# Planning the order of a fused attention and feed-forward kernel anew

## The chip, the cores and the metric

The kernel runs on one core of one Trainium2 chip. A core has five engines that run side by side and meet only through semaphores: TensorE (PE, matmuls into the accumulator memory, PSUM), VectorE (DVE), ScalarE (ACT), GpSimd (POOL) and SyncE (SP, which here issues every DMA). The metric is the device time of one execution in microseconds. The kernel before took 720.09 us, the median of three runs (719.34 to 721.42).

## The reference

Two stages follow each other; inputs and results are float32. B = 4, H = 8 heads, S = 1152 keys, D = 64, and the 1152 queries are averaged in pairs to 576.

```python
q_pool = q.reshape(B, H, S // 2, 2, D).mean(axis=3)
scores = (1 / np.sqrt(D)) * np.matmul(q_pool, k.transpose(0, 1, 3, 2))
scores = scores - np.max(scores, axis=-1, keepdims=True)
attn = np.exp(scores)
attn = attn / (np.sum(attn, axis=-1, keepdims=True) + 1e-09)
x = np.matmul(attn, v)             # heads side by side: (4, 576, 512)
h = np.maximum(x @ w_in, 0.0)      # (4, 576, 1024)
conv_out = conv_w[0] * h[t-1] + conv_w[1] * h[t] + conv_w[2] * h[t+1]
out = (h * sigmoid(conv_out)) @ w_out
```

## The kernel before

Heads are worked on in 16 pairs, four pairs to a batch. For a pair, keys, values and queries are loaded; GpSimd adds neighbouring queries; TensorE transposes keys and queries (L345, L350, L382, L392, into one of two accumulator buffers called `a`), and ScalarE copies them to `kt` and `qt`, the two heads on partitions 0 to 63 and 64 to 127. A DMA (L400) writes `qd`, the same queries with the two halves of the partitions swapped, so that a head's keys can be used from either half.

A score task (`scores`, L516) makes 128 queries by 1152 keys of one head in one of two buffers called `s`: 512 keys from one half of the partitions, 512 from the other, and the last 128. Each matmul in float32 is two instructions in the trace, so a task has six. VectorE takes the maximum (L528), ScalarE the exponential with its sum (L533), which frees the buffer. There are eight such tasks a pair, and a ninth (`m`) for the last 64 queries of both heads, with 64 by 64 blocks of the array. The exponentials, in `p`, are normalized and cut into a half-precision high part (ScalarE, L574) and low part (VectorE, L577), and a transposing DMA (L590) turns both. For the heads listed in `X32`, GpSimd normalizes instead (L607), TensorE transposes in float32 (L620) and ScalarE copies (L625). `values` multiplies by the values and sums over the keys: three half-precision products (L650) or one in float32 (L656) for every block of 128 keys, for 256 queries and then for 320; the list `BLOCK` gives the block of keys in which a row of values stands.

When a batch's four pairs are done, `feed` makes the first product (L690), rectifier (ScalarE), the three taps (GpSimd L699, VectorE L706), the gate, and `second` the second product (L749, and L755 for the last 64 rows). Its two parts of the tokens are interleaved with the next batch's attention. Weights come in through a chain of steps on VectorE, ScalarE and GpSimd.

The order in which every engine works is made by a planner. Each step is a `Task` with a key (its due time, in units of score tasks, from the table `AT`), an engine and a duration. `Plan.order` goes forward in time: of the steps that may begin, it takes the engine that is free first, and on it, of what could start within `LOOK` of the earliest, the one with the lowest key. `HOP` is the delay that it assumes between engines, `SWITCH` what a change of `mode` costs on TensorE, and steps with `port` set exclude each other. Tasks of one engine are then issued in that order, and the engine works through them strictly in turn.

## Time and profile before

| | |
|---|---|
| time of the runs | 719.34, 720.09, 721.42 us; median 720.09 |
| the profiled execution | 718.41 us, its span 716.6 us |
| TensorE, VectorE, ScalarE, GpSimd busy | 659.9, 551.2, 498.2, 177.1 us |
| TensorE's granted clock, mean over the span | 0.98 |
| DMA | 118.55 MB, its queue 79.8% of 16 engines' span |

The span is what the trace covers, from the first instruction to the last; the execution's own time lies around it. Busy time is a union: instructions of one engine that overlap count once. In the trace a matmul's record runs from its start to its modelled end, so the records of neighbours overlap.

### The profile page before, as it was taken

How to read it: one execution, taken by the hardware profiler on the slowest of the kernel's cores; microseconds unless marked ns; L12 is line 12 of the kernel's file. 1: busy time of each engine (PE TensorE's matmuls, PEld its weight loads, DVE VectorE, ACT ScalarE, POOL GpSimd, SP SyncE). 2: the span in 40 equal slices, each digit the busy share in tenths (PEclk: the TensorE clock that was granted, in tenths of full speed). 3: DMA queues.
4: the chain of work that ended last, by engine and by line, in shares of the span. 5: the costliest groups of instructions: out<-in, count | busy, mean ns of one | idle time of the engine just before them, and what ended most of it. 6: DMA issues, size and time to landing. Idle time of an engine off the chain costs nothing.

```text
span 716.6 us, 11043 instructions
## 1 busy us (share of the span) xinstructions
PE 659.9 (92%) x3992; PEld 398.6 (56%) x3992; DVE 551.2 (77%) x813; ACT 498.2 (70%) x810; POOL 177.1 (25%) x237
## 2 busy tenths in 40 slices
PE   4789889899998899999999998999999989999997
PEld 3445555556565545456665664456665655458743
DVE  2878887887889898868888999578888889864610
ACT  2887878876786777676876888567886868663310
POOL 2442453433433322011241212031141212001200
PEclk9999999999999899999999998999999999999999
DMA  5887695764468989989999999989999896873001
GB/s 155 221 178 179 167 212 132 166 167 118 113 141 173 233 151 190 209 186 202 200 183 221 193 182 223 193 172 175 220 181 209 161 187 144 171 168 74 1 30 37
DMA packets 311722, 118.55 MB, mean 165 GB/s; under 512 B 286556, under 2 KB 297332, under 8 KB 311668
## 3 DMA queue, kind: packets, MB, share of 16 engines
q1 hardware_dynamic: 311668, 117.85, 79.8%
q8 instruction: 31, 0.51, 0.3%
q14 instruction: 23, 0.19, 0.1%
HBM read 36.72 MB, written 4.72 MB: 58 GB/s over the span
## 4 chain that ended last, share of the span: by engine, by line
PE 68%; DVE 6%; ACT 5%; issue 2%; ACTq 0%; DVEq 0%
PE s L516 17%; PE a L690 17%; PE a L749 16%; PE a L650 12%; PE a L755 2%; DVE sm L528 2%; PE a L656 2%; DVE hl L577 2%; ACT p L533 2%; ACT hl L574 1%; PE a L620 1%; PE a L345 1%; PE a L426 1%; ACT pt L625 1%; PE a L382 0%
## 5 line engine op out<-in xcount | busy, mean ns | idle before, releaser
L528 DVE TENSOR_REDUCE sm<-s 128x1 f32<-128x1152 f32 x144 | 193.3, 1351 | 57.4 <-PE s L516 56.6
L533 ACT ACTIVATE p<-s,sm 128x1152 f32<-128x1152 f32 x144 | 175.4, 1219 | 49.4 <-DVE sm L528 41.3
L516 PE MATMUL s<-kt,qt 64*128 64x512 f32 (+3 forms) x512 | 184.0, 515 | 11.4 <-ACT p L533 10.7
L516 PE MATMUL s<-kt,qd 64*128 64x512 f32 (+2 forms) x448 | 177.9, 546 | 13.0 <-ACT p L533 11.5
L577 DVE SCALAR_TENSOR_TENSOR hl<-p,sm,hl 128x1152 f16<-128x1152 f32 (+1 forms) x124 | 176.9, 1437 | 11.8 <-ACT hl L574 10.7
L574 ACT ACTIVATE hl<-p,sm 128x1152 f16<-128x1152 f32 (+1 forms) x124 | 153.0, 1249 | 10.4 <-DVE sm L549 4.3
L690 PE MATMUL a<-x,wi 128*128 128x257 f32 (+1 forms) x512 | 140.1, 424 | 2.2 <-ACT pt L625 0.9
L749 PE MATMUL a<-wo,g 128*128 128x512 f32 x256 | 119.2, 607 | 0.6 <-ACT kt L354 0.6
L650 PE MATMUL a<-pt,v 128*64 128x256 f16 (+1 forms) x1458 | 118.2, 289 | 0.1
L516 PEld LDWEIGHTS s<-kt,qt 64*128 64x128 f32 (+1 forms) x512 | 70.8, 178 | 79.8 <-issue 59.1
L690 PEld LDWEIGHTS a<-x,wi 128*128 128x128 f32 x512 | 96.1, 194 | 33.9 <-issue 3.9
L699 POOL TENSOR_SCALAR g<-h,cw 128x255 f32<-128x255 f32 (+1 forms) x64 | 51.6, 809 | 231.2 <-ACT h L696 229.8
L516 PEld LDWEIGHTS s<-kt,qd 64*128 64x128 f32 (+1 forms) x448 | 65.8, 182 | 66.9 <-issue 44.2
L650 PEld LDWEIGHTS <-v 128*64 128x64 f16 x1458 | 90.7, 110 | 14.7 <-issue 5.2
L706 DVE SCALAR_TENSOR_TENSOR g<-h,cw,g 128x321 f32<-128x321 f32 (+1 forms) x128 | 66.8, 524 | 16.0 <-POOL g L699 14.6
L749 PEld LDWEIGHTS a<-wo,g 128*128 128x128 f32 x256 | 46.5, 192 | 50.7 <-issue 46.4
L696 ACT ACTIVATE h<-a 128x257 f32<-128x257 f32 (+1 forms) x64 | 26.2, 409 | 40.0 <-PE a L690 38.6
L656 PE MATMUL a<-pt,v 128*64 128x256 f32 (+1 forms) x180 | 48.6, 412 | 1.5 <-ACT pt L625 0.8
L625 ACT ACTIVATE pt<-a 128x384 f32<-128x384 f32 (+1 forms) x70 | 32.0, 477 | 17.5 <-PE a L620 16.8
L620 PE MATMUL a<-ident,p 128*128 128x128 f32 (+1 forms) x225 | 34.6, 275 | 5.1 <-ACT pt L625 2.4
L607 POOL TENSOR_SCALAR p<-p,sm 128x1152 f32<-128x1152 f32 (+1 forms) x25 | 32.1, 1285 | 28.9 <-DVE sm L549 23.1
L451 POOL TENSOR_SCALAR vs<-vs 128x1 f32<-128x1 f32 x16 | 9.3, 582 | 107.3 <-DVE vs L445 91.8
(68 smaller groups left out, 551.3 us busy)
## 6 DMA issues: line engine op xcount, KB each, us to landing
kin<-in_k_dram SPq DMA_DIRECT2D x16, 576.0 KB, 4.5
qin<-in_q_dram SPq DMA_DIRECT2D x32, 256.0 KB, 3.4
vin<-in_v_dram SPq DMA_DIRECT2D x11, 576.0 KB, 5.4
g<-in_moe_w_in_dram SPq DMA_DIRECT2D x8, 512.0 KB, 6.0
g<-in_moe_w_out_dram SPq DMA_DIRECT2D x8, 512.0 KB, 3.5
out_dram<-o SPq DMA_DIRECT2D x16, 256.0 KB, 2.5
qd<-qt SPq DMA_DIRECT2D x16, 160.0 KB, 3.4
pt<-hl SPq DMA_TRANSPOSE x135, 4.7
```

The costliest lines, as they stand in the source:

```text
L516: nc.tensor.matmul(out=w, lhsT=f, rhs=o.kt[r, e, c1:c2], start=True, stop=True)
L528: nc.vector.tensor_reduce(out=sm[:, e:e + 1], in_=runs(st[e]), axis=AX.XY, op=ALU.max, negate=True)
L533: nc.scalar.activation(out=p.tile().rearrange("p (a n) -> p a n", a=2), in_=runs(st[e]), func=AF.Exp, bias=sm[:, e:e + 1], scale=1.0, accu ...
L574: nc.scalar.activation(out=hl[rows, 0], in_=ps_[e][rows], func=AF.Copy, scale=sm[rows, 6 + e:7 + e])
L577: nc.vector.scalar_tensor_tensor(out=hl[rows, 1], in0=ps_[e][rows], scalar=sm[rows, 6 + e:7 + e], in1=hl[rows, 0], op0=ALU.mult, op1=ALU.s ...
L620: nc.tensor.transpose(w[:, (i - a1) * nq:(i - a1 + 1) * nq], ps_[e][rows, i * P:(i + 1) * P], ident[rows, rows])
L650: nc.tensor.matmul(out=to, lhsT=o.v[:, e, BLOCK[c], vc:vc + D], rhs=o.pt[y, e][:, hl * NC + c, 0:n], start=(c == 0 and j == 0), stop=(c == ...
L656: nc.tensor.matmul(out=to, lhsT=o.v[:, e, BLOCK[c]].bitcast(F32), rhs=p32.rearrange("p (a n) -> p a n", a=NC)[:, c, 0:n], start=(c == 0), ...
L690: nc.tensor.matmul(out=w[:, 0:n], lhsT=wi[:, j, f * P:(f + 1) * P], rhs=x.x[:, 255 * u:255 * u + n], start=(j == 0), stop=(j == KC - 1),)
L699: nc.gpsimd.tensor_scalar(out=g[:, f % 4, 0:tok], in0=h[:, 0:tok], scalar1=cw[:, f, 0:1], scalar2=1.0, op0=ALU.mult, op1=ALU.mult,)
L706: nc.vector.scalar_tensor_tensor(out=c, in0=h[:, t:t + tok], scalar=cw[:, f, t:t + 1], in1=c, op0=ALU.mult, op1=ALU.add)
L749: nc.tensor.matmul(out=w.tile(), lhsT=g[f // 4][:, f % 4, c:c + P], rhs=wo[:, f, :], start=(f == 0), stop=(f == FC - 1),)
```

## The change

The planner's table of durations is replaced, and with it the keys in `AT`. `HOP` goes from 0.12 to 0.19, a hop within TensorE from 0.03 to 0; the rule that two steps with `port` exclude each other is taken out; among the steps that could start, one of TensorE that stays in its mode counts as due 0.95 earlier. `HIGH` moves 16 of the high parts to GpSimd. `X32` gets one head of the eleventh pair. `values` is cut in two steps where it was cut in three.

A pair's keys are turned in nine transposes of 128 by 128: the 18 blocks of 64 columns of both heads are taken two by two, the ninth holding a block of either head. So `kt` has no second index, the second head's blocks stand in another order (`BLOCK` has one list a head), and the 128 last keys of the second head lie in the other half of the partitions than those of the first. The second head's score task therefore starts on partitions 64 to 127. The last queries are summed twice, side by side, and turned in one full transpose, so that they stand on both halves of the partitions; the swapped copy `qd` and its DMA leave them out, and the swap waits for the other queries alone.

```diff
-    HOP = 0.12
+    HOP = 0.19
...
-                at = max(t.ready, s[0], free.get(t.engine, 0.0), port if t.port else 0.0)
+                at = max(t.ready, s[0], free.get(t.engine, 0.0))
...
-                key=lambda c: (first[c[1].engine], c[1].rank),
+                key=lambda c: (
+                    first[c[1].engine],
+                    c[1].key - (AT["stay"] if c[1].engine == "PE" and c[1].mode == mode else 0.0),
+                    c[1].rank,
+                ),
...
-                hop = 0.03 if n.engine == t.engine and not t.dma else self.HOP
+                hop = self.HOP if n.engine != t.engine or t.dma else 0.0 if n.engine == "PE" else 0.12
...
-    "first_v": 1.35, "load": -15.29, "load_v": -7.7, "turn_k": -6.99, "turn_q": -4.19, "abs_v": -6.45,
...
+    "first_v": 1.88, "load": -3.54, "load_v": 0.5, "turn_k": -6.86, "turn_q": -6.9, "abs_v": -4.95,
...
+    "wi_step": 2.86, "wo": 31.13, "wo_step": 2.5, "stay": 0.95,
...
-HIGH = [0, 0, 0, 0, 0, 0, 0, 0, 0, 0, 0, 0, 0, 0, 0, 0]
-X32 = {(0, 0), (1, 0), (2, 0), (3, 0), (4, 0)}
+HIGH = [3, 0, 0, 0, 0, 0, 0, 3, 0, 1, 1, 4, 1, 0, 4, 2]
+
+BOTH = set()
+
+PARTS = 2
+X32 = {(0, 0), (1, 0), (2, 0), (3, 0), (4, 0), (10, 0)}
...
-    BLOCK = (0, 2, 4, 6, 8, 1, 3, 5, 7)
+    BLOCK = ((0, 2, 4, 6, 8, 1, 3, 5, 7), (2, 4, 6, 8, 0, 1, 3, 5, 7))
...
     r_vin = Ring("vin", 1, sb, [P, 2, NC, D], F32, lead=True)
     r_qin = Ring("qin", 1, sb, [P, 2, 2, 4, D], F32, lead=True)
     r_qm = Ring("qm", 1, sb, [P, 2, D], F32, lead=True)
-    r_kt = Ring("kt", 2, sb, [P, 2, K0], F32, lead=True)
+    r_kt = Ring("kt", 2, sb, [P, S], F32, lead=True)
     r_qt = Ring("qt", 2, sb, [P, K0], F32, lead=True)
-    r_qd = Ring("qd", 2, sb, [P, K0], F32, lead=True)
+    r_qd = Ring("qd", 2, sb, [P, K1], F32, lead=True)
     r_qs = Ring("qs", 1, sb, [P, 4, 2, D], F32, lead=True)
-    r_qms = Ring("qms", 1, sb, [P, D], F32, lead=True)
+    r_qms = Ring("qms", 1, sb, [P, 2, D], F32, lead=True)
     r_v = Ring("v", 2, sb, [P, 2, NC, P], F16, lead=True)
     r_p = Ring("p", 3, sb, [P, S], F32, lead=True)
     r_hl = Ring("hl", 4, sb, [P, 2, S], F16, lead=True)
...
             def turn(i=i, w=w):
-                if i < 2:
-                    for c in range(4):
-                        nc.tensor.transpose(
-                            w[:, c * P:(c + 1) * P], o.kin[:, i, 2 * c:2 * c + 2].rearrange("p c d -> p (c d)"), ident
-                        )
-                else:
-                    for e in range(2):
-                        nc.tensor.transpose(w[0:D, e * P:(e + 1) * P], o.kin[:, e, 8], ident)
+                rows = o.kin.tile().rearrange("p h c d -> p (h c d)")
+                for n, c in enumerate([range(0, 8, 2), range(10, 18, 2), (8,)][i]):
+                    nc.tensor.transpose(w[:, n * P:(n + 1) * P], rows[:, c * D:(c + 2) * D], ident)
 
             def keep(i=i, w=w):
-                if i < 2:
-                    nc.scalar.activation(out=o.kt[:, i, 0:K1], in_=w[:, 0:K1], func=AF.Copy)
-                else:
-                    nc.scalar.activation(
-                        out=o.kt[0:D, :, K1:K0], in_=w[0:D, 0:2 * P].rearrange("p (e n) -> p e n", e=2), func=AF.Copy
-                    )
-
-            t = add(k0 + AT["turn_k"] + i, "PE", 0.75 if i < 2 else 0.4, turn, after=lk,
+                n = K1 if i < 2 else P
+                nc.scalar.activation(out=o.kt[:, i * K1:i * K1 + n], in_=w[:, 0:n], func=AF.Copy)
+
+            t = add(k0 + AT["turn_k"] + i, "PE", 0.5 if i < 2 else 0.15, turn, after=lk,
                     uses=[o.kin] + ([o.kt] if i else []), takes=[w] if i else [w, o.kt])
             o.kts.append(
-                add(k0 + AT["turn_k"] + i + 0.1, "ACT", act(K1 if i < 2 else 2 * P), keep, after=[t],
-                    uses=[w, o.kt])
+                add(k0 + AT["turn_k"] + i + 0.1, "ACT", act(K1 if i < 2 else P), keep, after=[t], uses=[w, o.kt])
...
         def sum_m():
-            nc.gpsimd.tensor_tensor(out=o.qms.tile(), in0=o.qm[:, 0], in1=o.qm[:, 1], op=ALU.add)
+            for i in range(2):
+                nc.gpsimd.tensor_tensor(out=o.qms[:, i], in0=o.qm[:, 0], in1=o.qm[:, 1], op=ALU.add)
...
         def turn_m():
-            nc.tensor.transpose(wm[0:D, 0:P], o.qms.tile(), ident)
+            nc.tensor.transpose(wm[:, 0:P], o.qms.tile().rearrange("p i d -> p (i d)"), ident)
 
         def keep_m():
-            nc.scalar.activation(out=o.qt[0:D, K1:K0], in_=wm[0:D, 0:P], func=AF.Copy, scale=QSCALE)
+            nc.scalar.activation(out=o.qt[:, K1:K0], in_=wm[:, 0:P], func=AF.Copy, scale=QSCALE)
 
         def swap(e):
             h, g = slice(D - D * e, P - D * e), slice(D * e, D * e + D)
-            n = K1 if e else K0
-            nc.sync.dma_start(out=o.qd[h, 0:n], in_=o.qt[g, 0:n])
-
-        t0 = add(k0 + AT["sum_q"], "POOL", 0.95, lambda: sum_q(0), after=lq, uses=[o.qin], takes=[o.qs], port=True)
-        t1 = add(k0 + AT["sum_q"] + 0.1, "POOL", 0.95, lambda: sum_q(1), after=lq, uses=[o.qin, o.qs], port=True)
-        t2 = add(k0 + AT["sum_q"] + 0.2, "POOL", 0.4, sum_m, after=[lm], uses=[o.qm], takes=[o.qms], port=True)
-        t = add(k0 + AT["turn_q"], "PE", 0.75, turn_q, after=[t0, t1], uses=[o.qs], takes=[w, o.qt])
+            nc.sync.dma_start(out=o.qd[h], in_=o.qt[g, 0:K1])
...
-        sw = add(k0 + AT["turn_q"] + 0.3, "SP", 1.0, lambda: [swap(e) for e in range(2)], after=[tq, tm],
+        sw = add(k0 + AT["turn_q"] + 0.3, "SP", 1.0, lambda: [swap(e) for e in range(2)], after=[tq],
...
         def scores(ends):
-            for half, c1, c2, at in ((0, 0, K1, 0), (1, 0, K1, 2 * 512), (0, K1, K0, 512)):
+            for main in (0, 1, 2):
                 for e in ends:
+                    half = 1 - e if main == 1 else e
                     r = slice(D * half, D * half + D)
                     if m:
-                        f = (o.qd if half else o.qt)[r, K1 + D * e:K1 + D * e + D]
+                        f = o.qt[r, K1 + D * e:K1 + D * e + D]
                     else:
                         f = (o.qt if half == e else o.qd)[r, d * P:(d + 1) * P]
                     t = st[0 if m else e].tile()[slice(D * e, D * e + D) if m else slice(0, P)]
-                    if at == 512:
+                    if main == 2:
                         w = t[:, 512:1024].rearrange("p (a n) -> p a n", n=D)[:, 0:8:7, :]
+                        kk = o.kt[r, 2 * K1:S]
                     else:
-                        w = t[:, at:at + 512]
-                    nc.tensor.matmul(out=w, lhsT=f, rhs=o.kt[r, e, c1:c2], start=True, stop=True)
+                        w = t[:, 1024 * main:1024 * main + 512]
+                        kk = o.kt[r, e * K1:e * K1 + K1]
+                    nc.tensor.matmul(out=w, lhsT=f, rhs=kk, start=True, stop=True)
...
-            for c in range(3 * i, 3 * i + 3):
+            for c in range(NC * i // PARTS, NC * (i + 1) // PARTS):
...
-                                out=to, lhsT=o.v[:, e, BLOCK[c], vc:vc + D], rhs=o.pt[y, e][:, hl * NC + c, 0:n],
+                                out=to, lhsT=o.v[:, e, BLOCK[e][c], vc:vc + D], rhs=o.pt[y, e][:, hl * NC + c, 0:n],
```

The order at the start, on TensorE, first the kernel before (`kin`: keys, `qs`: queries, `qms`: last queries, `s`: scores, made from `qt` or the swapped `qd`):

```order
L345 MATMUL a<-ident,kin 128x128 x8
L350 MATMUL a<-ident,kin 64x128 x2
L382 MATMUL a<-ident,qs 128x128 x4
L392 MATMUL a<-ident,qms 64x128
L516 MATMUL s<-kt,qt 128x512
L516 MATMUL s<-kt,qd 128x512
L516 MATMUL s<-kt,qt 128x2x64
L516 MATMUL s<-kt,qd 128x512
L516 MATMUL s<-kt,qt 128x512
L516 MATMUL s<-kt,qd 128x2x64
```

and of the changed kernel:

```order
L379 MATMUL a<-ident,qs 128x128 x4
L351 MATMUL a<-ident,kin 128x128 x4
L389 MATMUL a<-ident,qms 128x128
L351 MATMUL a<-ident,kin 128x128 x5
L515 MATMUL s<-kt,qt 128x512
L515 MATMUL s<-kt,qd 128x512
L515 MATMUL s<-kt,qt 128x2x64
L515 MATMUL s<-kt,qt 128x512
L515 MATMUL s<-kt,qd 128x512
L515 MATMUL s<-kt,qt 128x2x64
```

The queries now stand ahead of the keys, the last queries between the keys, and the second score task no longer begins with the swapped queries.

In the fourth batch, on TensorE, where the third batch's second product is filled in between score tasks; the kernel before, in the batch's last pair:

```order
L749 MATMUL a<-wo,g 128x512 x8
L516 MATMUL s<-kt,qd 128x512
L516 MATMUL s<-kt,qt 128x512
L516 MATMUL s<-kt,qd 128x2x64
L749 MATMUL a<-wo,g 128x512 x2
L516 MATMUL s<-kt,qt 128x512
L516 MATMUL s<-kt,qd 128x512
L516 MATMUL s<-kt,qt 128x2x64
L749 MATMUL a<-wo,g 128x512 x2
```

and the changed kernel, in the batch's second pair:

```order
L753 MATMUL a<-wo,g 128x512 x2
L351 MATMUL a<-ident,kin 128x128 x4
L515 MATMUL s<-kt,qt 128x512
L515 MATMUL s<-kt,qd 128x512
L515 MATMUL s<-kt,qt 128x2x64
L515 MATMUL s<-kt,qt 128x512
L515 MATMUL s<-kt,qd 128x512
L515 MATMUL s<-kt,qt 128x2x64
L389 MATMUL a<-ident,qms 128x128
L753 MATMUL a<-wo,g 128x512 x2
L351 MATMUL a<-ident,kin 128x128 x4
```

Score tasks stood one by one between matmuls of another shape, and now also stand two by two; the transposes stand beside the second product, in the same shape.

At the end, on TensorE, behind the last sums over keys; the kernel before:

```order
L690 MATMUL a<-x,wi 128x257 x4
L690 MATMUL a<-x,wi 128x323 x16
L690 MATMUL a<-x,wi 128x257 x4
L690 MATMUL a<-x,wi 128x323 x16
L749 MATMUL a<-wo,g 128x512 x32
L755 MATMUL a<-wo,g 64x256 x16
```

and the changed kernel, from the last sums over 256 queries on (the 108 rows of the last sums over 320 stand behind the eighth row below):

```order
L759 MATMUL a<-wo,g 64x256 x4
L694 MATMUL a<-x,wi 128x257 x4
L759 MATMUL a<-wo,g 64x256 x4
L694 MATMUL a<-x,wi 128x257 x4
L759 MATMUL a<-wo,g 64x256 x4
L694 MATMUL a<-x,wi 128x257 x4
L759 MATMUL a<-wo,g 64x256 x4
L694 MATMUL a<-x,wi 128x257 x12
```

The 16 half-width matmuls of the third batch's second product alternate with the first product of the fourth; before they stood as twelve and four around the sums over 256 queries.

## Rows read from the trace of the kernel before

**Rows 1.** The page's busy times by engine: us, share of the span, instructions.
```profile
PE 659.9 (92%) x3992; PEld 398.6 (56%) x3992; DVE 551.2 (77%) x813; ACT 498.2 (70%) x810; POOL 177.1 (25%) x237
```

**Rows 2.** Busy time of each engine in six stretches of the span. Columns: the stretch, its length, the engines in the order PE, PEld, DVE, ACT, POOL with their instructions, PE's granted clock, DMA share, GB/s.
```profile
14.88:144.74 129.86, 112.88 (x735) 69.16 (x735) 104.70 (x157) 106.25 (x185) 53.40 (x60) 0.97 0.77 182
144.74:322.64 177.90, 162.78 (x951) 97.53 (x951) 150.40 (x232) 130.42 (x216) 49.77 (x63) 0.97 0.78 167
322.64:480.73 158.09, 153.15 (x966) 91.50 (x965) 132.09 (x185) 118.38 (x182) 31.52 (x47) 0.98 1.05 196
480.73:635.84 155.11, 149.02 (x949) 89.55 (x948) 132.43 (x181) 115.23 (x175) 30.17 (x36) 0.99 0.94 183
635.84:716.60 80.76, 76.30 (x381) 47.67 (x380) 28.61 (x56) 23.18 (x48) 9.09 (x18) 0.99 0.19 47
```

**Rows 3.** The waits of all engines, the row of TensorE's score tasks for ScalarE's exponentials: us in total, times, longest us.
```profile
PE s L516 <- ACT p L533: 22.2, 24, 2.8
```

**Rows 4.** The chain that ended last, in order of time: start us, us, what (instructions merged).
```profile
377.21 2.35 PE s L516 x11
...
456.74 1.91 PE a L749 x4
458.66 1.27 PE s L516 x6
459.93 3.63 PE a L749 x8
...
598.40 3.07 PE a L650 x54
```

**Rows 5.** TensorE's timeline in one score task that begins at 609.74: start us, us, engine, line, operation, array shape, tile, count.
```profile
610.27 0.59 PE L516 MATMUL s<-kt,qd 64*128 64x512 f32 x1
...
610.70 0.38 PE L516 MATMUL s<-kt,qd 64*128 64x128 f32 x2
```

**Rows 6.** TensorE's timeline from 196 to 216, a pair in which one head is in float32 (columns as in rows 5).
```profile
197.64 0.38 PE L656 MATMUL a<-pt,v 128*64 128x256 f32 x1
...
197.85 0.38 PE L656 MATMUL a<-pt,v 128*64 128x256 f32 x1
...
206.74 0.60 PE L345 MATMUL a<-ident,kin 128*128 128x128 f32 x4
```

**Rows 7.** The page's costliest groups, the low and the high parts: busy us, mean ns of one, then idle time before them.
```profile
L577 DVE SCALAR_TENSOR_TENSOR hl<-p,sm,hl 128x1152 f16<-128x1152 f32 (+1 forms) x124 | 176.9, 1437 | 11.8 <-ACT hl L574 10.7
L574 ACT ACTIVATE hl<-p,sm 128x1152 f16<-128x1152 f32 (+1 forms) x124 | 153.0, 1249 | 10.4 <-DVE sm L549 4.3
```

**Rows 8.** The page's DMA issues, the transposes: count, us from issue to landing.
```profile
pt<-hl SPq DMA_TRANSPOSE x135, 4.7
```

**Rows 9.** The timelines of GpSimd and of VectorE from 100 to 130 us (columns as in rows 5; idle time before in brackets).
```profile
101.35 1.47 POOL L376 TENSOR_TENSOR qms<-qm 128x64 f32<-128x64 f32 x1
...
101.23 1.42 DVE L577 SCALAR_TENSOR_TENSOR hl<-p,sm,hl 128x1152 f16<-128x1152 f32 x1 [1.05 <-ACT hl L574]
...
108.24 0.17 DVE L545 TENSOR_SCALAR sm<-sm 128x2 f32<-128x2 f32 x1 [0.81 <-ACT p L533]
...
126.05 1.04 DVE L545 TENSOR_SCALAR sm<-sm 128x2 f32<-128x2 f32 x1
```

**Rows 10.** All instructions of one line: shortest, median and longest in ns, first and last start. GpSimd's sum of the last queries and its normalization.
```profile
L376 POOL TENSOR_TENSOR qms<-qm x16: 316/322/1473, 9.2 to 545.4; 128x64 f32<-128x64 f32 x16
L607 POOL TENSOR_SCALAR p<-p,sm x25: 1218/1228/2232, 22.0 to 206.0; 128x1152 f32<-128x1152 f32 x20, 64x1152 f32<-64x1152 f32 x5
```

**Rows 11.** The timeline of all engines from 0 to 22 us (columns as in rows 9).
```profile
3.65 1.41 POOL L370 TENSOR_TENSOR qs<-qin 128x256 f32<-128x256 f32 x2 [2.11 <-DMA qin<-in_q_dram]
...
7.73 1.94 PE L345 MATMUL a<-ident,kin 128*128 128x128 f32 x8 [7.73 <-DMA kin<-in_k_dram]
8.85 0.60 ACT L354 ACTIVATE kt<-a 128x512 f32<-128x512 f32 x1 [6.84 <-PE a L345]
...
10.45 1.09 PE L382 MATMUL a<-ident,qs 128*128 128x128 f32 x4 [0.31 <-ACT kt L354]
10.46 0.65 ACT L811 ACTIVATE g<-g 128x512 f32<-128x512 f32 x1
...
11.57 0.63 ACT L385 ACTIVATE qt<-a 128x512 f32<-128x512 f32 x1 [0.46 <-PE a L382]
...
12.10 0.25 ACT L395 ACTIVATE qt<-a 64x128 f32<-64x128 f32 x1
...
12.37 1.18 SPq L400 DMA_DIRECT2D qd<-qt  x2
...
14.88 1.22 PE L516 MATMUL s<-kt,qd 64*128 64x512 f32 x1 [0.55 <-DMA qd<-qt]
```

**Rows 12.** TensorE's timeline from 634 to 717 us, the last score task, of the last queries (columns as in rows 5).
```profile
635.84 0.65 PE L516 MATMUL s<-kt,qt 64*64 64x512 f32 x2
...
636.32 0.59 PE L516 MATMUL s<-kt,qt 64*64 64x512 f32 x2
```

More of the change, by code (lines that the diff above doesn't have):

```diff
@@ L84, in order @@
         mode = 0
-        port = 0.0
         dma = 0.0
@@ L158, in order @@
             free[t.engine] = busy
-            if t.port:
-                port = busy
             t.end = busy
@@ L522, in softmax @@
         ex, ps_ = [], []
+        both = n == 2 and o.k0 // 9 in BOTH
+        if both:
+            mm = add(i0 + AT["mm"], "PE", 2.05, lambda: [scores((e,)) for e in range(2)], after=o.kts + o.qts, mode=1,
+                     uses=[o.qt, o.qd, o.kt], takes=st)
         for e in range(n):
@@ L549, in inverse @@
             nc.vector.reciprocal(out=sm[:, 6:6 + n], in_=sm[:, 4:4 + n])
-        iv = add(i0 + n + AT["inv"], "DVE", 0.3, inverse, after=ex, uses=[sm])
+        iv = add(i0 + n + AT["inv"], "DVE", 0.27, inverse, after=ex, uses=[sm])
         y = int(d > 1)
@@ L580, in low @@
                     )
-                t = add(i0 + n + e + AT["high"], "POOL" if on_pool else "ACT", 1.35 if on_pool else act(S, 0.1), high,
+                t = add(i0 + n + e + AT["high"], "POOL" if on_pool else "ACT", 1.2 if on_pool else act(S, 0.13), high,
                         after=[iv], uses=[ps_[e], sm], takes=[hl], port=on_pool)
-                t = add(i0 + n + e + AT["low"], "DVE", dve(S) + 0.05, low, after=[t], uses=[ps_[e], sm, hl], port=True)
+                t = add(i0 + n + e + AT["low"], "DVE", dve(S) + 0.035, low, after=[t], uses=[ps_[e], sm, hl], port=True)
             for h in by_dma:
@@ L610, in norm @@
                     )
-                td = add(i0 + n + e + AT["high"], "POOL", 1.35, norm, after=[iv],
+                td = add(i0 + n + e + AT["high"], "POOL", 1.25, norm, after=[iv],
                          uses=[sm, ps_[e]] + ([] if new else [pt]), takes=[pt] if new else [], port=True)
@@ L667, in values @@
         t = None
-        for i in range(3):
-            t = add(key + 0.1 * i, "PE", (n * 9.0 / 2400 + 0.02) * (4 / 3 if any(o.x32) else 1), lambda i=i: part(i), mode=2,
+        for i in range(PARTS):
+            t = add(key + 0.1 * i, "PE", (n * 27.0 / PARTS / 2400 + 0.02) * (4 / 3 if any(o.x32) else 1), lambda i=i: part(i), mode=2,
                     after=o.turned[y] + o.vls + ([t] if t else []),
@@ L722, in feed @@
             t = add(key + 0.5, "ACT", act(n), relu, after=[t], uses=[w], takes=[h])
-            t = add(key + 0.6, "POOL", gp(tok), tap0, after=[t] + cw_ready, uses=[h] + ([] if first else [g]),
+            t = add(key + 0.6, "POOL", gp(tok) + 0.02, tap0, after=[t] + cw_ready, uses=[h] + ([] if first else [g]),
                     takes=[g] if first else [], port=True)
@@ L726, in feed @@
             t = add(key + 1.1, "DVE", dve(tok), lambda tap=tap: tap(2), after=[t], uses=[h, g], port=True)
-            t = add(key + 1.5, "ACT", act(tok), tanh, after=[t], uses=[g])
-            done.append(add(key + 2.0, "DVE", dve(tok), gate, after=[t], uses=[h, g], port=True))
+            t = add(key + 1.5, "ACT", act(tok, 0.04), tanh, after=[t], uses=[g])
+            done.append(add(key + 2.0, "DVE", dve(tok) - 0.06, gate, after=[t], uses=[h, g], port=True))
         return gs, done
```

50 lines of the change are left out of this document (27 added, 23 removed).

## The prediction

> **What bounds the kernel now.** I read the busy shares first: TensorE is busy for 659.9 of 716.6 us, VectorE for 551, ScalarE for 498, GpSimd for 177 [rows 1]. A mean hides stages, so next comes the table by stretch, cut at the first complete score task, at the last score task of every fourth pair, and at the end [rows 2]. In the last 80.76 us TensorE works alone (76.30 busy, VectorE 28.61). From 322.64 to 635.84 it is busy for 302.2 of 313.2 us. In the two stretches before that it is idle for 17.0 and 15.1 us, and there VectorE reaches 81% and 85%. The waits say for whom it was idle: 22.2 us in 24 waits for the exponentials that free one of the two score buffers [rows 3]. So TensorE sets the pace nearly everywhere, with a latency loop behind it in the first half. The profiled execution took 718.41 us, 1.8 more than its span; the median shown, 720.09, is 1.7 above that.
>
> What a stretch of TensorE costs is read off the chain [rows 4]. Four matmuls of the second product take 1.91 us, eight take 3.63: 0.43 each, and 0.19 that is paid once. A score task takes 1.27 between other work, two in a row 2.35. Work in one array shape thus costs its columns, and each change of shape 0.19 us.
>
> **The change part by part.**
>
> *Fewer changes of shape.* Counting rows of TensorE that follow each other in one array shape (weight loads left out), I find 356 such stretches before and 278 after: 349 against 265 up to the last score task, 7 against 13 behind it. The key and query transposes that came out on 64 partitions are gone, sums over keys that were cut in three (rows of 18) mostly run whole, and score tasks stand side by side more often. 78 x 0.19 = -14.8 us. Lower bound 0, if each saved change only becomes idle time; the rows show no reason for more than the full sum.
>
> *Scores side by side.* In one task the two 512-column halves run at once and the 128 columns come last, alone, on the first half's rows [rows 5]: what follows a 512-column matmul starts 0.43 later, so 128 columns cost 0.11, and there are two of them, 0.21 us. Before, the next task begins on the same rows and must queue behind them. Now the second head begins on the other half, so these 128 columns run beside its first 512. This pays only where two tasks touch: 25 times after (80 alone, 22 twos, a four). The three at the start I leave out: 22 x 0.21 = -4.6 us; between 0 and -5.3.
>
> *Head (10, 0) goes the full-precision way.* It adds 36 + 9 transposes. Four transposes last 0.60 us [rows 6], of which 0.19 is the change already counted and the rest columns: 0.10 each, half of it for the small ones, +4.1 us. Its sums over keys are 18 instructions for 256 queries that start 0.21 to 0.22 apart [rows 6], 3.9 us, where 54 half-precision ones in pairs take 3.07 - 0.19 = 2.9 [rows 4]; by the columns 4.8 against 3.6 for 320. +2.2 us. Together +6.3. In exchange four of 124 low parts of 1.44 us leave VectorE, five high parts of 1.25 ScalarE, and five of 135 DMA transposes the queue [rows 7, 8]. None is a term: they lay beside TensorE's work, but they give the new pace room.
>
> *Nine key transposes for ten:* 16 x 0.10 = -1.6 us. The last-queries transpose keeps its columns, and the second GpSimd sum (16 x 0.32 us, the usual length [rows 10]) is hidden behind loads issued a pair ahead; if that cover goes, TensorE meets it once a pair, +5 us.
>
> *16 high parts move from ScalarE to GpSimd:* ScalarE loses 16 x 1.25 = 20 us that did not set the end; GpSimd gains 16 x 1.23 [rows 7, 10], with the five new normalizations and the sums 31 us in all, and then has about 208. No term, but a rival below.
>
> *The start.* Before, the first score task waits at 14.88 for the swapped queries, whose DMA was issued at 12.37 behind keys and queries [rows 11]. Now the query transposes stand first: sums end at 3.65 + 1.41 = 5.06, transposes and copy take 1.09 + 0.63, so the swap, which no longer waits for the last queries, is issued near 6.9 and is there 2.5 later, at 9.4. Late next are the keys: they land at 7.73; from 8.85, where ScalarE made its first copy, it has a key copy 0.60, last queries 0.25, one step of the weights 0.65 and two key copies, 0.9. So 11.3: 14.88 - 11.3 = -3.6 us. At worst 0 (the weights' step in that queue waits for its own load), at best -4.5.
>
> *The tail.* Behind the last score task stand four rows more of the second product (3.4 us that the body loses) and six changes of shape more, already in the count. It shifts work, the sum stays.
>
> *The new order.* The body's idle time, 17.0 + 15.1 + 4.9 + 6.1 = 43 us, is not fixed: the planner no longer keeps GpSimd and VectorE apart, counts 0.19 for a hop where it counted 0.12, and prefers to stay in a shape. No row prices that. I take 0, with 13 us (30% of the idle time) either way.
>
> Sum: -14.8 - 4.6 + 6.3 - 1.6 - 3.6 = -18.3. 718.4 - 18.3 = 700.1; the median shown lies 1.7 above the profiled execution, so 701.8. I predict 702.
>
> **Two places where a rule stands against it.** The last-queries task: before, its two heads read the same rows at a time, and all four quarters of the array run at once, 0.65 for the first, the next 0.48 later [rows 12]. After, the two heads write one buffer bank from different row halves at the same time, on different partitions. The trace has two row halves only in different banks, so it does not decide. The Trainium skill (TensorEngine Tiling (Array Packing), Gotcha 1: PSUM Pressure) says that different row tiles cannot access the same PSUM bank simultaneously.
>
> The port: a GpSimd sum of usually 0.32 us [rows 10] took 1.47 when it began inside a VectorE step, and ended with that; a VectorE step that takes 0.17 elsewhere took 1.04 [rows 9], while GpSimd worked. The Trainium skill (SBUF — State Buffer, Who interferes with whom) calls what the two share an exclusive lock: whichever starts first holds it for its whole instruction. The trace agrees, and the old planner kept such steps apart where the new one does not.
>
> **The rivals.**
> 1. *The new order also takes out idle time.* For it: ScalarE and VectorE lose some 20 and 6 us, and a planner whose durations are nearer to the rows should wait less. Against: the loop through two score buffers is as long as before. A third of the 43 us gone: 702 - 14 = 688. Chance 0.22.
> 2. *What TensorE gains turns into idle time in the first half,* because there the loop of scores, maximum and exponential sets the pace. Of the 84 changes saved before the last score task 42 lie before the eighth pair's end: 42 x 0.19 = 8, with the side-by-side scores there some 10 us lost: 712. Chance 0.13.
> 3. *The last-queries tasks serialize,* since their two heads write one bank from two row halves. Two heads one after the other: 2 x 0.43 + 2 x 0.11 = 1.08 more, 16 times, 17 us: 719, no change. Against it: the outputs lie on different partitions. This is what that rule of the Trainium skill on row tiles and banks would come to. Chance 0.05.
> 4. *Slower: GpSimd and VectorE block each other.* Place: every VectorE step that starts while GpSimd reads, some 570 instructions that are not reductions over scores. If they fell at random, GpSimd busy for 0.29 of the time with steps of 1.23 us would cost each 0.29 x 0.6, together 99 us. VectorE has, at the new pace, a slack of about 68 us in the last twelve pairs (491 us before, less 14, against 415 - 6 busy); it decides from there, and the remaining 31 us go on top: 733. Against it: the old trace is not random either, the low parts' mean is 1.44 [rows 7] where one takes 1.42 [rows 9], though GpSimd worked for a quarter of that time. Chance 0.10.
>
> **How the numbers follow.** The forecast itself (692 to 712) has 0.50. About 0.3% is what a measurement can tell from no change, so 718 to 722 is the same. Faster: 0.50 + 0.22 + 0.13 = 0.85. Same 0.05. Slower 0.10. The range reaches through rivals 1 and 2: down to 684, where 40% of the idle time goes (702 - 17), and up to 717, where half of the changes of shape and of the side-by-side scores (9.7) and the start (3.6) give nothing and the order loses 2 us more.
>
> **What would show it.** TensorE's busy time near 645; the first complete score task near 11.3; the last stretch from the last score task to the end near 85; a last-queries task still 1.27 between other work (2.3 would be rival 3); two neighbouring score tasks 2.14 where they took 2.35. VectorE's low parts with a mean above 1.6 and more waits of ScalarE for them would be rival 4. A TensorE busy time that falls while its idle time in the first 323 us grows by as much is rival 2. I am wrong if TensorE's busy time does not fall.

## The result and the profile after

The changed kernel takes 697.25 us (median of 4 runs, 695.88 to 700.81). The kernel before, run beside it, takes 719.75 (719.34 to 721.42). The ratio is 0.969, with a 95% interval of 0.965 to 0.973: faster by 22.5 us, where 18 were forecast. The profiled execution after took 695.88 us, its span is 694.1, that is 22.5 us less than before. Of the runs below one, of e4_always_two, took 1052.9 us at a granted clock of 0.60 and is left out of that kernel's row.

First the busy line of the page, which answers to [rows 1]:

```profile
PE 645.4 (93%) x4003; PEld 402.1 (58%) x4003; DVE 568.4 (82%) x808; ACT 476.8 (69%) x804; POOL 228.7 (33%) x275
```

TensorE is busy 14.5 us less, so it is idle for 48.7 us instead of 56.7. ScalarE is busy 21.4 us less, GpSimd 51.6 more, and VectorE 17.2 more although it has five instructions fewer.

The same by stretch, cut where [rows 2] cut: at the first score task, at the last one of every fourth pair, at the end (columns as there).

```profile
0.00:10.06 10.06, 3.97 (x15) 2.42 (x15) 0.00 (x0) 2.84 (x5) 2.95 (x17) 1.00 0.71 217
10.06:143.04 132.98, 111.28 (x724) 69.76 (x723) 124.42 (x174) 108.03 (x193) 64.08 (x66) 0.96 0.77 184
143.04:301.70 158.66, 147.81 (x934) 93.27 (x934) 148.19 (x213) 121.19 (x204) 61.35 (x66) 0.99 0.80 172
301.70:458.50 156.80, 153.09 (x993) 96.37 (x995) 130.25 (x181) 114.63 (x189) 50.46 (x61) 1.00 0.92 185
458.50:609.41 150.91, 148.56 (x959) 91.60 (x955) 133.73 (x185) 106.47 (x169) 41.22 (x47) 1.00 0.91 182
609.41:694.10 84.69, 80.73 (x389) 48.66 (x388) 31.83 (x58) 23.61 (x48) 8.64 (x18) 1.00 0.28 60
```

Against [rows 2] the start is 4.8 us shorter (14.88), the second stretch 3.1 longer, the third 19.2 shorter, the next two 1.3 and 4.2 shorter, the tail 3.9 longer, since four rows of the second product and more moved into it. The column before the last two is the granted clock. A stretch at the lower of the two levels (1.2 GHz) counts 0.5 in it, so the time at that level is twice what is missing to 1: before, 0.06 x 129.86 + 0.06 x 177.9 + 0.04 x 158.09 + 0.02 x 155.11 = 28 us, after 0.08 x 132.98 + 0.02 x 158.66 = 14 us. So part of TensorE's 14.5 us is clock and not work. In the stretches whose granted clock reads 0.50, TensorE is busy for 25.0 us before and 13.1 after. With these halved, its work is 647.4 us before and 638.9 after (an estimate from the two traces; "work" below is meant so). The 22.5 us are then about 8.5 of work, 5.9 of clock and 8.0 of idle time, 3.0 of them before the first score task. This is an account of two executions and not of causes: where TensorE is slower it also waits less, so not all of the 5.9 need be time lost.

The waits after, four rows (us in total, times, longest). [rows 3] answers to the third.

```profile
POOL g L703 <- ACT h L700: 138.0, 48, 14.9
ACT p L536 <- DVE sm L531: 64.4, 56, 3.5
PE s L515 <- ACT p L536: 22.0, 22, 3.5
DVE sm L531 <- PE s L515: 17.6, 19, 2.3
```

And the row of before that belongs to the last of them:

```profile
DVE sm L528 <- PE s L516: 56.6, 57, 4.0
```

TensorE waits for the exponentials as long as before. But VectorE's maxima now wait 17.6 us for scores, where they waited 56.6: VectorE turned from an engine with slack into one that is nearly full in the first 300 us (124.42 of 132.98 and 148.19 of 158.66).

### The profile page after: what moved, and what is told of

Its sections match the earlier page's. It is cut to its first block, busy times and chain, and to the rows that moved or that the text cites. A ratio compares the mean times of both kernels' runs of the same rounds, so it can differ in the third digit from the quotient of the medians.

```text
span 694.1 us, 11095 instructions
## 1 busy us (share of the span) xinstructions
PE 645.4 (93%) x4003; PEld 402.1 (58%) x4003; DVE 568.4 (82%) x808; ACT 476.8 (69%) x804; POOL 228.7 (33%) x275
## 5 line engine op out<-in xcount | busy, mean ns | idle before, releaser
L536 ACT ACTIVATE p<-s,sm 128x1152 f32<-128x1152 f32 x144 | 175.8, 1221 | 83.4 <-DVE sm L531 64.4
L531 DVE TENSOR_REDUCE sm<-s 128x1 f32<-128x1152 f32 x144 | 192.9, 1348 | 17.7 <-PE s L515 17.6
L581 DVE SCALAR_TENSOR_TENSOR hl<-p,sm,hl 128x1152 f16<-128x1152 f32 (+1 forms) x120 | 176.0, 1479 | 13.7 <-ACT hl L578 6.7
L515 PEld LDWEIGHTS s<-kt,qt 64*128 64x128 f32 (+1 forms) x704 | 92.4, 175 | 125.9 <-issue 83.0
L515 PE MATMUL s<-kt,qd 64*128 64x512 f32 x256 | 146.9, 656 | 0.0
L578 ACT ACTIVATE hl<-p,sm 128x1152 f16<-128x1152 f32 (+1 forms) x104 | 129.5, 1251 | 10.3 <-DVE sm L553 5.1
L694 PE MATMUL a<-x,wi 128*128 128x257 f32 (+1 forms) x512 | 134.2, 413 | 1.2 <-ACT h L700 0.7
L654 PE MATMUL a<-pt,v 128*64 128x256 f16 (+1 forms) x1404 | 117.7, 288 | 0.1
L694 PEld LDWEIGHTS a<-x,wi 128*128 128x128 f32 x512 | 94.1, 189 | 32.0 <-issue 2.9
L654 PEld LDWEIGHTS <-v 128*64 128x64 f16 x1404 | 88.9, 110 | 12.6 <-issue 4.1
L710 DVE SCALAR_TENSOR_TENSOR g<-h,cw,g 128x255 f32<-128x255 f32 (+1 forms) x128 | 70.9, 557 | 26.2 <-POOL g L703 24.4
L611 POOL TENSOR_SCALAR p<-p,sm 128x1152 f32<-128x1152 f32 (+1 forms) x30 | 41.7, 1390 | 52.0 <-DVE sm L553 40.2
L660 PE MATMUL a<-pt,v 128*64 128x256 f32 (+1 forms) x216 | 55.2, 409 | 0.3 <-ACT pt L629 0.3
L624 PE MATMUL a<-ident,p 128*128 128x128 f32 (+1 forms) x270 | 41.0, 277 | 7.3 <-POOL p L611 3.0
L366 POOL TENSOR_TENSOR qs<-qin 128x256 f32<-128x256 f32 x32 | 28.2, 895 | 56.4 <-PE a L379 53.3
L716 ACT ACTIVATE g<-g 128x255 f32<-128x255 f32 (+1 forms) x64 | 27.8, 441 | 27.2 <-DVE g L710 27.0
L629 ACT ACTIVATE pt<-a 128x384 f32<-128x384 f32 (+1 forms) x84 | 38.1, 479 | 10.3 <-PE a L624 9.7
```

The source lines that it names most:

```text
L515: nc.tensor.matmul(out=w, lhsT=f, rhs=kk, start=True, stop=True)
L531: nc.vector.tensor_reduce(out=sm[:, e:e + 1], in_=runs(st[e]), axis=AX.XY, op=ALU.max, negate=True)
L536: nc.scalar.activation(out=p.tile().rearrange("p (a n) -> p a n", a=2), in_=runs(st[e]), func=AF.Exp, bias=sm[:, e:e + 1], scale=1.0, accu ...
L578: nc.scalar.activation(out=hl[rows, 0], in_=ps_[e][rows], func=AF.Copy, scale=sm[rows, 6 + e:7 + e])
L581: nc.vector.scalar_tensor_tensor(out=hl[rows, 1], in0=ps_[e][rows], scalar=sm[rows, 6 + e:7 + e], in1=hl[rows, 0], op0=ALU.mult, op1=ALU.s ...
L611: nc.gpsimd.tensor_scalar(out=ps_[e][rows], in0=ps_[e][rows], scalar1=sm[rows, 6 + e:7 + e], scalar2=2.0 ** -14, op0=ALU.mult, op1=ALU.mult,)
```

## Two readings of the clock

Runs of one kernel differ in the mean clock that each lists, and the time goes with it. Over all runs of this study, within each kernel, 0.01 of mean clock less goes with 3.6 us more (45 runs of the kernel before: 3.4, from 0.970 with 720.85 us to 0.986 with 715.46). So each experiment below has its median and also its time at a clock of 0.985, worked out with that slope from the means of its runs. This is a correction by what goes together, not an experiment: a kernel that waits more may draw the lower clock itself, and then the clock is part of its price. Kernel by kernel the slope runs from 1.3 to 5.5 us (8.7 in e4), so corrected times that lie 1 us apart say little.

| kernel | median us | ratio to before [95%] | mean clock | at 0.985 |
|---|---|---|---|---|
| before (45 runs) | 718.39 to 719.43 (three medians) | | 0.979 | 716.6 |
| changed (4) | 697.25 | 0.969 [0.965, 0.973] | 0.986 | 698.2 |
| e1_halves (6) | 701.3 | 0.976 [0.972, 0.981] | 0.981 | 699.9 |
| e2_new_code_old_plan (6) | 710.32 | 0.988 [0.985, 0.992] | 0.988 | 710.9 |
| e3_new_plan_old_code (6) | 707.31 | 0.985 [0.982, 0.988] | 0.981 | 706.1 |
| e4_always_two (5) | 734.01 | 1.022 [1.018, 1.026] | 0.962 | too far |
| e5_late_start (6) | 704.3 | 0.978 [0.975, 0.982] | 0.981 | 701.5 |
| e6_ports_apart (12) | 712.01 | 0.991 [0.989, 0.994] | 0.976 | 709.3 |
| e7_five_heads (6) | 698.16 | 0.972 [0.969, 0.975] | 0.982 | 697.4 |
| e8_high_on_scalar (12) | 716.53 | 0.996 [0.994, 0.999] | 0.971 | 711.5 |
| e9_high_in_place (6) | 706.53 | 0.982 [0.979, 0.985] | 0.981 | 704.8 |
| e10_three_steps (5) | 710.08 | 0.989 [0.987, 0.991] | 0.977 | 707.5 |
| e12_keys_first (5) | 699.25 | 0.975 [0.972, 0.977] | 0.981 | 699.1 |

At one clock the change is worth 716.6 - 698.2 = 18.4 us.

## The experiments

**Code and plan apart.** Two kernels: the new code (nine transposes, last queries in one, swap before the last queries, score halves side by side) under the old planner and its table; and the new planner, table and options with the old code.

```
-AT = {"first_v": 1.88, "load": -3.54, ...      e2: the old table, HOP 0.12, port rule, five heads, PARTS 3
+    if i < 2: ... else: nc.tensor.transpose(w[0:D, e * P:(e + 1) * P], ...)   e3: the old turns, rings, swap, scores
```

> The kernel before with the new transposes, halves and swap, but the old planner, its table, X32 and three steps of sums. Theory: 316 stretches of one shape against 356 (-7.6 us), 12 touching tasks (-2.5), one transpose a pair less (-1.6): 720 - 12 = 708. Rival (order alone): 719 to 721. Third (old code was the whole of it): 697.

> The changed kernel with the new planner and table, one step after the other as it is, but the old ten key transposes, old halves, and a swap that waits for the last queries. Theory: 315 stretches against 278 (+7.0 us), 23 touching tasks (+4.8), 16 transposes (+1.6), a later start (+2): 697 + 15 = 712. Rival (order alone): 697 to 699.

Measured 710.32 and 707.31. At one clock the code is worth 5.7 us under the old plan (716.6 - 710.9) and 7.9 under the new (706.1 - 698.2), the plan 10.5 on the old code and 12.7 on the new. By the medians it is 9 to 10 and 12 to 13. Both halves are needed, they nearly add, and the plan is the larger one. TensorE's stretches in one shape number 316 and 315 in these two, against 356 before and 278 after: each half takes some 40 of them away. But of the new code's 40 (under the old plan) and 37 (under the new) 36 each lie between a transpose that came out on 64 partitions and work in 128*128, by a count over the traces, and that change costs nothing where it is measured below. Without those 36 the two expectations come to 0.8 + 2.5 + 1.6 = 4.9 us for the code under the old plan, where 5.7 were measured at one clock, and to 0.2 + 4.8 + 1.6 + 2 = 8.6 under the new, where 7.9 were; as written they were 12 and 15.

**Scores side by side.** The halves are put back into an order in which neighbours meet on the same rows; the order of the work is that of the changed kernel.

```
-            for main in (0, 1, 2):
+            for main in (0, 1, 2) if m else (1, 0, 2):
```

> The changed kernel with its order kept; only within a score task the 512 keys of the other half are issued first, so that every task begins on the half of the rows on which the one before it ended. Theory (TensorE's work sets the end): 23 touching tasks lose 0.21 us each, +4.8 us, 702; TensorE busy near 650, two tasks in a row 2.35 instead of 2.14. Rival (the gain is the order's alone, the halves are hidden): 697, unchanged.

The chain of the changed kernel, then the row of this one's that answers to its first (start us, us, what), then the last-queries task of the kernel before:

```profile
600.36 2.14 PE s L515 x10
602.50 3.79 PE a L654 x54
606.29 1.27 PE s L515 x6
607.56 1.92 PE a L753 x4
609.48 1.22 PE s L515 x12
```

```profile
608.41 2.25 PE s L515 x10
```

```profile
635.91 1.23 PE s L516 x12
```

Two touching tasks take 2.14 us, as predicted, against 2.35 in [rows 4]. The edit brings back only half of it, 2.25: with the halves in that order one run of 128 columns is in the way, not two. So 22 x 0.11 = 2.4 us were to come back, and at one clock 1.7 did; TensorE's work grew by 1.5 (640.4). The 4.1 us between the medians have clock in them (0.976 in the profiled run, where the changed kernel has 0.990). The last-queries task took 1.23 before and takes 1.22 (609.48 above); the 1.27 that the prediction gives for it is that of an ordinary score task.

**The start.** In the first pair alone the queries are turned behind the keys and the swap waits for the last queries, as before.

```
-        t = add(k0 + AT["turn_q"], "PE", 0.5, turn_q, after=[t0, t1], ...
+        tq0 = AT["turn_q"] if o is not pairs[0] else AT["turn_k"] + 2.5
+        t = add(k0 + tq0, "PE", 0.5, turn_q, after=[t0, t1] + (o.kts if o is pairs[0] else []), ...
-        sw = add(k0 + AT["turn_q"] + 0.3, "SP", 1.0, ..., after=[tq],
+        sw = add(k0 + tq0 + 0.3, "SP", 1.0, ..., after=[tq] + ([tm] if o is pairs[0] else []),
```

> The changed kernel; for the first pair alone the queries are turned behind all keys and the swap waits for the last queries, as before; the rest of TensorE's order is the same. Theory (the start is a term of its own): the first maximum begins near 16.7 instead of 13.1 and the whole is 3.6 us later, 701. Rival (the delay is caught up in the first pairs, where TensorE has idle time): 697 to 698.

The timeline of the changed kernel's start (start us, us, engine, line, operation, idle before), which answers to [rows 11]:

```profile
5.84 0.62 ACT L382 ACTIVATE qt<-a 128x512 f32<-128x512 f32 x1 [3.82 <-PE a L379]
6.48 1.16 SPq L396 DMA_DIRECT2D qd<-qt  x2
...
10.00 0.66 ACT L815 ACTIVATE g<-g 128x512 f32<-128x512 f32 x1 [0.62 <-DMA g<-in_moe_w_in_dram]
...
10.06 1.22 PE L515 MATMUL s<-kt,qt 64*128 64x512 f32 x1
...
13.14 1.35 DVE L531 TENSOR_REDUCE sm<-s 128x1 f32<-128x1152 f32 x1
```

and one row of the experiment:

```profile
16.53 1.36 DVE L532 TENSOR_REDUCE sm<-s 128x1 f32<-128x1152 f32 x1 [2.38 <-PE s L516]
```

The swap is issued at 6.48 instead of 12.37, and the first maximum is 3.4 us later in the experiment. At one clock the whole is 3.3 us longer: here what the start loses is lost in full. By the medians it is 7.0, and the rest goes with the clock: of its six runs two have 0.990 and 699.38 and 700.2 us, the other four 0.973 to 0.981 and 703.75 to 705.69. The changed kernel's two runs at 0.990 took 695.88 and 696.86, 3.4 us less than those two. In its profile, though, idle time is 49.1 us in all, only 0.4 more than in the changed kernel, and e12 below is a late start that cost little.

**Always two score tasks at once.** Would it pay to let all tasks touch?

```
-BOTH = set()
+BOTH = set(range(16))
```

> The changed kernel, planned with the two heads' score tasks always as one step: 217 stretches of one shape instead of 278, 64 touching pairs instead of 25. If TensorE's work alone set the end: -11.6 - 8.2 = 677, TensorE busy near 626. Rival (the loop through two score buffers): TensorE's busy time falls so, but it idles for the exponentials by at least as much more, since both buffers must be free at once: 697 or more, the wait of score tasks for exponentials above 60 us (22 now).

Slower than before, though TensorE's stretches in one shape fall to 217 and two tasks touch 64 times. Its work does fall, to 624.8 us, 14.1 below the changed kernel's, where 19.8 were counted. Three of its waits, and its second stretch by engine:

```profile
ACT p L536 <- DVE sm L531: 81.6, 65, 4.1
...
DVE sm L549 <- ACT p L536: 42.1, 32, 4.0
...
PE s L515 <- ACT p L536: 17.2, 17, 3.0
```

```profile
10.06:150.00 139.94, 111.50 (x668) 71.81 (x668) 121.17 (x171) 103.32 (x182) 61.03 (x65) 0.85 0.72 174
```

The rival that expected a stalled loop holds in its time, not in its row: TensorE's own wait is shorter than in the changed kernel. ScalarE waits 81.6 us for maxima (64.4 in the changed kernel) and the inverse of the sums 42.1 us for the second exponential (7.4 there), which fits two buffers that are taken at once. TensorE is idle for 81 us, and in the second stretch the granted clock is 0.85: some 42 of 140 us at the lower level. Fewer changes of shape were worth nothing here, where the loop through the two buffers grew longer. But this kernel too was planned anew (see below), so not all of the loss need be the loop's.

**What a change of shape costs.** In every group of the first product in the last half batch, two transposes are put ahead that nothing reads, 128*128 in one group and 128*64 in the next.

```
+                if b == B - 1 and u == 1:
+                    for _ in range(2):
+                        if f % 2: nc.tensor.transpose(w[0:D, 0:P], ident[:, 0:D], ident)
+                        else: nc.tensor.transpose(w[:, 0:P], ident, ident)
```

> The changed kernel with two idle transposes ahead of each of the last batch's eight second-half groups of the first product, by turns 128 by 128 (the same shape) and 128 by 64 (another shape); their outcome is overwritten. There TensorE never waits. Theory (each change of shape costs 0.19): a group of the other shape takes 0.38 us longer than one of the same. Rival (a change beside short matmuls costs less than the 0.19 read beside long ones): 0.15 to 0.25 longer.

The chain in that place (L698 is 128*128, L696 is 128*64), and TensorE's weight loads there (start us, us):

```profile
640.39 0.22 PE a L698 x2
640.61 2.18 PE a L700 x8
642.78 0.22 PE a L696 x2
643.00 2.18 PE a L700 x8
```

```profile
640.34 1.93 PEld L700 LDWEIGHTS a<-x,wi 128*128 128x128 f32 x8
642.35 0.11 PEld L696 LDWEIGHTS a<-ident 128*64 128x64 f32 x1
642.62 0.11 PEld L696 LDWEIGHTS a<-ident 128*64 128x64 f32 x1 [0.17 <-issue]
642.73 1.93 PEld L700 LDWEIGHTS a<-x,wi 128*128 128x128 f32 x8
```

2.40 us in either case, so the change to these 64-column transposes and back costs 0.00 us: both expectations miss. The loads stand ahead of their matmuls and are hidden. The transposes of the kernel before do the same: at 209.04 the first of L350 (128*64) starts 0.11 us after the last of L345 (128*128), as those of L345 do among themselves.

That does not hold for every change between 128*128 and 128*64. In the tail of the changed kernel the last 64 rows of the second product (L759, 128*64, whose matmuls run in pairs, one on each half of the columns) alternate with the first product (L694). Its chain there, and then one load and its matmul:

```profile
616.05 3.07 PE a L654 x54
619.12 0.86 PE a L759 x8
619.98 1.93 PE a L694 x8
621.91 1.01 PE a L759 x8
...
628.82 5.40 PE a L694 x24
```

```profile
622.86 1.16 PEld L694 LDWEIGHTS a<-x,wi 128*128 128x128 f32 x6 [0.39 <-issue]
```

```profile
622.86 1.35 PE L694 MATMUL a<-x,wi 128*128 128x257 f32 x5
```

Eight of L759 take 0.86 us behind L654, which has their shape, and 1.01 behind L694. Eight of L694 take 1.93, where sixteen more cost 3.47, that is 1.74 for eight. So a change costs 0.15 to 0.19 us here, and the load begins only with its matmul. The shape that the trace prints therefore does not decide the price; in these rows it is paid where the next weights are not loaded ahead. The rule of the Trainium skill (TensorEngine Tiling (Array Packing), Key Properties) that changing the tiling mode drains TensorE does not show in the transposes and agrees with the tail; whether the transposes change the mode at all, the trace does not say. The 0.19 us of [rows 4] was read beside score tasks, whose arrays have 64 rows, and there it still stands: 1.92 for four matmuls of the second product, where four more cost 1.72.

**The 16 high parts, in place.** The order of the changed kernel is kept; the high parts that it gives to GpSimd are done by ScalarE at the same place.

```
-                    if on_pool:
-                        nc.gpsimd.tensor_scalar(out=hl[rows, 0], ...)
-                        return
                     nc.scalar.activation(out=hl[rows, 0], ...)
```

> The changed kernel in its own order; the 16 high parts of GpSimd are put, at the same places of the plan, on ScalarE. Theory (ScalarE's 20 us did not set the end): 697 to 700. Rival (they stand in the loop of scores, maximum and exponential, as the slow run with all high parts planned on ScalarE would say): 705 or more, more waits for exponentials than 22 us.

9.3 us by the medians, 6.6 at one clock. The wait that grew, first as the changed kernel has it, then as this one:

```profile
DVE hl L581 <- ACT hl L578: 6.7, 10, 2.5
DVE hl L581 <- POOL hl L573: 6.0, 6, 1.4
```

```profile
DVE hl L575 <- ACT hl L572: 19.4, 24, 2.5
```

VectorE waits 19.4 us for high parts instead of 12.7. TensorE's work is the same (639.0 us); it is idle for 53.3 us instead of 48.7, and in this profile it has 32 us at the lower level instead of 14. ScalarE is busy for 70% and is nowhere the bound by share, yet its 16 instructions cost time in this order. That they do so through the loop of scores, maximum and exponential is not shown: the rival's own sign did not come, for score tasks wait 22.7 us for exponentials, hardly more than the 22.0 before. An order made for ScalarE might pay less.

**Edits with a new plan each.** Four kernels change one option and let the planner order everything anew: its port rule back (GpSimd and VectorE kept apart), head (10, 0) back to half precision, all high parts on ScalarE, sums over keys in three steps.

```
+                at = max(t.ready, s[0], free.get(t.engine, 0.0), port if t.port else 0.0)   e6
-X32 = {(0, 0), (1, 0), (2, 0), (3, 0), (4, 0), (10, 0)}
+X32 = {(0, 0), (1, 0), (2, 0), (3, 0), (4, 0)}                                              e7
-HIGH = [3, 0, 0, 0, 0, 0, 0, 3, 0, 1, 1, 4, 1, 0, 4, 2]
+HIGH = [0] * 16                                                                             e8
-PARTS = 2
+PARTS = 3                                                                                   e10
```

> The changed kernel, planned with the old rule that steps of VectorE and GpSimd on their common port exclude each other. Theory (the lock costs VectorE time but does not set the end): VectorE's busy time falls from 568 towards 550, the time is 697 to 706, for the keys were chosen without the rule. Rival (the lock holds the new kernel back): 692 or less.

> The changed kernel without the sixth float32 head (10, 0), planned again with the same table. Theory (TensorE's work alone): 6.3 us less of it, 281 stretches, 691. Rival (the head is worth its transposes, since it takes low parts, high parts and DMA transposes out of a stretch where they set the pace): 697 or more.

> The changed kernel with all high parts on ScalarE, planned again. Theory (TensorE's work alone): 261 stretches instead of 278 and six touching tasks more, -4.5, 693. Rival (ScalarE's 20 us stand in the loop of scores, maximum and exponential): more waits for exponentials (22 us now), 700 or more.

> The changed kernel with the sums over keys in three steps, planned again with the same table: 265 stretches instead of 278. Theory (fewer stretches is less time): -2.5, 695. Rival (keys chosen for one plan lose when it is made again, whatever is changed): 705 or more, with TensorE's idle time above 55 us (48.7 now).

Measured 712.01, 698.16, 716.53 and 710.08. e10 is the warning: its stretches fall to 265, fewer than the changed kernel's 278, and its work to 635.0 us, yet it is slower by 13 us, with 55.7 us of idle time and 41 us at the lower level. The table of numbers fits one order, and a slight edit can throw the planner into another that is 9 to 13 us worse at one clock (e10 9.3, e6 11.1, e8 13.3); e7 shows that it need not. So e6, which lies outside both of its ranges, and e8 cannot be put down to their edits alone. What e6 does show is its busy line:

```profile
PE 650.3 (92%) x4003; PEld 404.6 (57%) x4003; DVE 548.2 (77%) x808; ACT 478.4 (67%) x804; POOL 215.9 (30%) x275
```

VectorE is busy 20.2 us less and GpSimd 12.8 less than in the changed kernel: that is about what the two block each other there, by the count below. The kernel is slower all the same, and whether the changed kernel would gain without the blocking stays open. e7 takes 6.3 us of TensorE's work away by the prediction's count, 7.0 by its trace (631.9), and is as fast as the changed kernel (697.4 against 698.2 at one clock), with 3.8 us more of idle time.

**Keys before weights.** In ScalarE's first rows the last key copies go before the weights' first step, which waits 0.62 us for its load in the timeline above.

```
+    order[first:last + 1] = kept + held      the weights' first step, and what waits for it, behind the key copies
```

> The changed kernel with one row moved: at the start ScalarE copies the last keys before it begins the weights' first step, not behind it. Theory (the start is a term of its own): the first maximum begins near 12.1 instead of 13.1, and the whole is 1 us earlier, 696. Rival (caught up later): 697.

699.25 us, 699.1 at one clock: no gain shown. In its profile the key transposes began 0.9 us later, when the keys had landed, and the first maximum began at 15.35, not before 13.14, so the run doesn't settle what the place of that step is worth. It does show that a late start need not be lost in full: that execution, 2.2 us later at the first maximum, took 698.77 us at 0.985, 0.6 more than the changed kernel at that clock.

## Why the prediction was right

The time lies inside the range and 4.8 us below the forecast; at one clock the gain is 18.4 us, where the sum was 18.3. Point by point the sum is less good than that, and the closeness is in part luck. TensorE's busy time of 645.4, where 645 was named, is luck too: 5.9 of its fall of 14.5 us are clock.

- **Scores side by side, -4.6:** right in mechanism and size. 2.35 became 2.14, and the half of it that an edit took back cost 1.7 of 2.4 us.
- **The start, -3.6:** right. The first maximum began at 17.00 and begins at 13.14; undone it costs 3.3 to 3.4 at one clock. The swap was issued at 6.48 where 6.9 was worked out.
- **The tail:** 84.69 us, where 85 was named.
- **Fewer changes of shape, -14.8:** the step that failed. The count of 78 was right; the price of 0.19 was put on every one. Of them 36 lie between 128*128 work and a transpose that came out on 64 partitions, and that change costs 0.00. What is left, 42 x 0.19 = 8.0 us, agrees with TensorE's work: it fell 8.5, and with the other terms of work as predicted (-4.6 + 6.3 - 1.6 = 0.1) the changes took 8.6, not 14.8. The two kernels with code and plan apart say the same.
- **Head (10, 0), +6.3:** TensorE's work for it is there (7.0 less without it), but no cost in time was found (e7); since that kernel was planned anew, the term is neither confirmed nor refuted.
- **16 high parts to GpSimd, no term:** wrong. In place they are worth 6.6 to 9.3 us. That they "did not set the end" was said without a row for it; by which wait they cost TensorE time stays open.
- **The new order, 0 with 13 either way:** it gave. Idle time between the first score task and the tail fell from 43.1 to 38.6 us, and there is the clock, which no term held: 14 us less at the lower level, 5.9 by the account above, 3.6 by the slope. What of the plan's 10 to 13 us is high parts, changes of shape, idle time and clock stays open, since no edit of the plan leaves the rest of it alone.

So 6 us too much for the changes of shape stood against 4 to 5 of idle time and 4 to 6 of clock that were put at nothing.

The rivals. *Idle time taken out* happened to a tenth of the 43 us, not a third. *The gain turned into idle time in the first half* did not: 21.7 + 10.9 = 32.6 us there after, 32.1 before. *The last-queries tasks serialize* falls: 1.22 us against 1.23 before, with two heads that write one bank from two row halves. The Trainium skill's sentence that different row tiles cannot access the same PSUM bank at the same time (TensorEngine Tiling (Array Packing), Gotcha 1: PSUM Pressure) does not show as a price here, with outputs on different partitions. *GpSimd and VectorE block each other* happened in part. The low parts, to be read against [rows 7]:

```profile
L581 DVE SCALAR_TENSOR_TENSOR hl<-p,sm,hl 128x1152 f16<-128x1152 f32 (+1 forms) x120 | 176.0, 1479 | 13.7 <-ACT hl L578 6.7
```

1479 ns, where 1437 were before and 1600 would have spoken for the rival. Over all its work VectorE lost about 24 us: it has some 6.6 us less to do (four low parts of 1.44 us, one step of the values of 0.84) and is busy 17.2 more. That agrees with the lock that the Trainium skill names (SBUF — State Buffer, Who interferes with whom). But the rival counted 99 us against a slack of 68 (on some 570 steps, where 813 - 144 = 669 are not reductions over scores); the 24 stand beside 39 us less in which VectorE waited for scores (56.6 us then, 17.6 now).

## What to carry to other kernels

Read the price of a change of shape beside the very neighbours for which it is counted: here the same number was right around score tasks and zero around transposes on 64 partitions, and the sum came out only because other terms were left at nothing. A share of busy time does not clear an engine: 16 instructions moved to one that was busy for 69% cost 6.6 us or more (e9). Where a planner with fitted numbers sets the order, freeze the order to test an edit (e1, e9): an edit that is planned anew (e10) measures the planner too.

## What was not expected of the hardware

- Of the changes between 128*128 and 128*64 some cost nothing (2.40 us per group with either kind of transpose, the weight loads ahead) and some 0.15 to 0.19 us (L759 and L694 in the tail, the load beginning with its matmul), while four matmuls after a score task cost 0.19 more than their columns.
- Runs of one binary differ in the granted clock (0.970 to 0.986 in the kernel before) and by 3.4 to 3.6 us per 0.01 of it. The lower level is found mostly where TensorE waits: in the changed kernel in the stretch in which it is idle for 21.7 of 133 us (0.96) and hardly behind it, and in the kernel with the longest waits at 0.85. That a stall draws the lower level and so costs more than its length would fit the late start (3.4 us at equal clock, 7.0 by the medians), but is not shown.
- VectorE was busy some 24 us longer than its work would take in a kernel that became 22.5 us faster; it had been waiting 56.6 us for the bound.
